# A second written-out order for the engines of an attention and feed-forward kernel, nine more unread products, and one weight block copied by ScalarE

## The chip, the cores and the metric

The kernel runs on one core of a Trainium2 chip. The metric is the device time of one launch in microseconds (us). TensorE does the matrix products, VectorE and ScalarE elementwise work, GpSimd elementwise work and the transfers that add, and SyncE issues the plain transfers.

## The reference

Two parts follow each other. The first is attention over 4 batches of 8 heads, 768 positions and 64 features, in which each query sees the keys less than 16 positions away and, for each block of 32 positions, one summary key (the maximum) with one summary value (the mean).

```python
k_sum = k.reshape(B, H, nb, block, D).max(axis=3)
v_sum = v.reshape(B, H, nb, block, D).mean(axis=3)
scores_all = np.concatenate([scores_l_m, scores_s], axis=-1)   # near keys (masked), then summaries
a = softmax(scores_all)                                        # 1e-9 added to the sum
attn = a @ np.concatenate([v, v_sum], axis=2)
```

The second is a layer of width 2048 with a rational activation on the 3072 x 512 result.

```python
h = x @ w_in
g = (a0 + a1*h + a2*h**2 + a3*h**3) / (1 + |b0|*|h| + |b1|*h**2 + 1e-6)
out = g @ w_out
```

The spread of the inputs is wide, so the kernel carries the operands of the two large products as a high and a low part, and does three products where one would stand.

## The kernel before, in words

**Attention** is done in 48 chunks of 64 queries (names ending in 0 to 47: `sc3`, `ss3`, `pt3`, `pts3`, `av3`). Chunks 0 to 15 go through `early_half` (line 323). Scores of a pair of chunks are made by TensorE (`sc`). VectorE takes the maximum, ScalarE the exponentials (four activations, each with the read of its sum, and one small one), VectorE the reciprocal, GpSimd multiplies (four operations, `ss`; VectorE for chunks 3 and 5), TensorE transposes (`pt`), one engine copies (`pts`), TensorE multiplies by the values (`av`), and `xh` and `xl`, the high and low part of the result, are written by two more operations. `BYDVE` names the copies that VectorE does in place of ScalarE (`C3`: `pts` of chunk 3; `X3`: `xh` of chunk 3). Chunks 0 to 7 need the block means of the values: TensorE sums them (`vs`), ScalarE copies the sums beside chunk 0's values (`vw0`, four copies), and ScalarE and GpSimd copy them on for the other seven chunks (`first_means`, line 253).

**The two layers** run in 96 steps: 6 groups of 512 rows by 16 weight blocks. In a step TensorE does twelve products of the first layer (`h`: high part of x, low part, then the high part with the weights' low part; step 0 does the low part of x last). A dozen operations of ScalarE, VectorE and GpSimd then make the activation: `gh`, its high part, comes from VectorE, and `gl`, its low part, is the last and comes from GpSimd. Three steps later (`LAG`) twelve products of the second layer (`po`) use both. "Step 5's second layer" below is the twelve `po` products that read `gh0_5` and `gl0_5`.

**Weights** come as 64-bit numbers in 16 blocks of 1 MB (`wr0` to `wr15`) through SyncE and pass six stages in `w_split` (line 480): ScalarE scales, GpSimd turns one byte, VectorE joins the bits, then the high part is copied, and the low part is made. `MODE` has a letter per block for the last two: with `c` ScalarE copies and VectorE subtracts; with `b` a converting transfer of GpSimd copies, ScalarE negates and an adding transfer of GpSimd makes the low part; `e` is the same with the copy on ScalarE. Blocks 2, 6, 7, 8, 10 and 11 use an adding transfer. It stands in GpSimd's list of work and needs some us to land.

**Order.** Each engine does its work strictly in the order of the text, and that order is the token list `ORDER`: `a3` is the next stage of chunk 3, `b1` a pair's scores, `v` and `m` the means, `w8` the next stage of weight block 8, `h`, `g`, `q`, `P` the parts of a step, `K`, `Q`, `V`, `A`, `W` the transfers. `SLOTS` says which of a tile's buffers each use takes, and was made for that list. `VSP` names the PSUM bank of the two sums of means.

**Unread products.** `FILL` puts products that nobody reads ahead of a chunk's scores (`b`) or transposes (`t`) on TensorE; they are 480 columns of bf16, written to the bank that the chunk then overwrites.

Of the kernel before, what the change touches and what calls it, by code (L numbers as in the profile page):

```python
# [57 lines left out]
FILL = {'b0': 3, 'b4': 3, 't2': 5, 't0': 5}  # L58
SLOTS = {'wm': '1010', 'ta': '10101010101010101010101010101010101010101010101010101010101010101010101010101010101010101010101010', 'tq': '01101010101010101010101010101010100101010101010101101010101010101010101010101010101010110101010101', 'st': '010101010111100110011011', 'gh': '012011201201201201201201201201201201201201201201201201201201201201201201201201021021021021021201201201', 'h': '01010101010101010101010101010101010100100100101010101010101101100110101010100101001001010101001010110101101010101010101010', 'ks': '0101', 'o': '012301231032101320132013201320132013201', 'gl': '0120201201201201201201201201201201201201201201201201201201201201201201201201201201201201201201201201', 'sm': '012301320132102310321032103213012301231023102301', 'p': '0123201302301320133231023232313012131012031230202023010312101302012010131230313231203132132132303101021302130', 'xl': '0101010', 'tu': '010101010101010101010101010101010101010101010101010101010101010101010101010101010101010101010101010', 'a': '0101010101011011011001010100100101011101111010101001000100000011111011010101011101010010001011101111010010101010101010101010101010', 'xh': '0110101', 'pts': '010100101010100111010111011010100101011010100100', 'vs': '01'}
# [9 lines left out]
K1 Q0 K0 K3 S K2 W0 w0 d3 d0 w0 d1 d2 b0 a1 a0 Q1 a1 w0 W1 a1 a0 w0 a1 w1 B I b2 a4 b3 a0 a2 a4 W2 w1 a0 a2 w0 a7 F w1 c a4 V7 V4 a1 V3 b1 a2 w2 V6 w0  # L69
w1 a5 V5 a1 w2 w1 a2 a4 V0 w2 a7 w1 a0 v4 v5 v6 a7 k9 a5 v0 a6 V2 a7 v3 V1 A9 v8 v2 A8 a6 w2 v7 a0 v1 v9 m0 a3 a2 W3 a3 a0 w2 a5 a5 W5 m4 a4 m2 a6 m5  # L70
a2 k8 m3 a6 a0 b4 W4 a0 a4 a3 m1 a5 a5 a3 a9 w3 a1 a3 a1 a8 a5 a6 a3 a3 a7 a8 m6 a1 a6 w3 a7 G a2 w3 V8 a5 a2 a3 a8 w5 a4 a6 m7 w2 a7 a6 a6 a5 a2 a4
w5 a3 a7 w3 w4 a9 w3 a7 a4 a8 h0 V9 w5 g0 w4 w4 L11 h1 w3 a9 w5 n4 n3 g0 W6 q0 g0 w4 q0 W7 g1 w5 n0 w5 g0 A10 n1 a9 a8 a9 a8 a9 g1 g1 g0 q1 q1 g0 g1
g1 A11 h2 g2 W9 a9 g2 w4 q2 w4 W8 n2 n5 o P3 a9 g2 w6 q2 g1 a9 g2 h3 w6 g3 D11 a8 w6 w7 g2 w7 w6 g3 a8 g2 w6 w9 h4 P4 L10 q3 a8 w7 V11 g4 b5 P5 q3 a10
q4 g4 g3 g3 g3 w8 w6 h5 q4 w9 a11 w7 g4 w8 h6 g3 A12 a10 g5 P6 w8 g4 g4 g5 q5 w9 w8 g4 w7 w7 L13 W10 a11 q5 a11 P7 g5 w10 D10 w8 g5 V10 a10 h7 w10 g5
g6 w10 w10 a11 D13 q6 g6 w8 g5 w9 g6 w9 q6 L12 w9 a11 w10 g6 a10 P8 a10 g7 a10 a11 g6 w10 g6 W11 A13 h8 w11 g7 q7 a10 D12 a11 q7 w11 a10 W12 g7 P9 a10
g8 w12 w11 a11 g7 g7 k12 h9 W13 k13 q8 g8 w11 g7 q8 w12 g8 a11 w11 w12 w11 g9 g8 g8 P10 g8 w12 W15 g9 b6 A14 w13 h10 A15 w13 a13 g9 a13 q9 a12 q9 w13
# [700 lines left out]
```

## Time and profile before

| | us |
|---|---|
| median of 3 runs | 631.09 (631.05 to 631.6) |
| profiled execution | 630.29 |
| its span, first to last instruction | 628.4 |
| TensorE busy in the span | 615.1 |
| VectorE busy | 556.5 |
| ScalarE busy | 453.4 |
| GpSimd busy | 251.2 |

The span is what the rows below divide; 1.9 us of the execution lie around it. The first product of the first layer starts at 40.06 us. Before it chunks 0 to 7 of the attention are done, beside the first weights; after it TensorE runs the 96 steps with the rest of the attention between them.

### The profile page before, as it was taken

The page shows a single profiled execution, that of the slowest core. Times are in us where ns is not written, and L with a number is a line of the kernel's source. Part 1 is how long each engine was busy: PE and PEld are TensorE (multiplying, and loading weights), DVE is VectorE, ACT ScalarE, POOL GpSimd, SP SyncE. Part 2 cuts the span into 40 slices and gives each one's busy share as a digit, 9 for nine tenths or more (in the row PEclk, how much of TensorE's full clock was granted, in tenths as well). Part 3 has the DMA queues.
Part 4 walks back from the last instruction along what each step waited for, and adds up shares of the span by engine and source line. Part 5 has one row for each costly group of instructions (what it writes and reads, how often), then busy time and mean ns, then how long its engine had stood idle before and what let it go on. Part 6 is the DMA issues. An engine that isn't in the chain of part 4 may idle for free.

```text
span 628.4 us, 12096 instructions
## 1 busy us (share of the span) xinstructions
PE 615.1 (98%) x4204; PEld 491.8 (78%) x4204; DVE 556.5 (89%) x1068; ACT 453.4 (72%) x1007; POOL 251.2 (40%) x351
## 2 busy tenths in 40 slices
PE   8899989999999999999999999999999999999997
PEld 4577767778888888878888888888888887878885
DVE  4999999999999898899887999999798897867895
ACT  3998989777968677867785777858777675846553
POOL 0974664771424622334353133354143532221231
PEclk9799999999999999999999999999999999999999
DMA  8998799313342740423353433434413122100001
GB/s 331 340 310 329 221 263 284 118 32 103 121 148 83 213 126 18 159 86 119 111 164 101 143 92 113 145 101 134 136 55 105 59 65 74 68 0 2 0 1 67
DMA packets 52180, 80.78 MB, mean 129 GB/s; under 512 B 6472, under 2 KB 33000, under 8 KB 50200
## 3 DMA queue, kind: packets, MB, share of 16 engines
q1 hardware_dynamic: 50328, 74.87, 36.6%
q0 software_dynamic: 1424, 4.92, 3.5%
q8 instruction: 33, 0.54, 0.4%
q10 hardware_dynamic: 368, 0.22, 0.1%
q14 instruction: 27, 0.22, 0.1%
HBM read 60.33 MB, written 14.75 MB: 119 GB/s over the span
## 4 chain that ended last, share of the span: by engine, by line
PE 79%; DVE 9%; ACT 4%; DMA 3%; POOL 2%; issue 1%; SPq 0%; POOLq 0%; DVEq 0%; ACTq 0%
PE po L162 35%; PE h L162 35%; PE sc L162 4%; PE av L162 4%; DVE tu L162 3%; DVE tq L162 2%; ACT ta L162 2%; DMA w<-wr 1%; PE pt L162 1%; DVE gh L162 1%; DMA kres<-in_kraw_dram 1%; POOL gl L162 1%; DVE wr L162 1%; DMA kr<-in_kraw_dram 1%; DVE sm L162 1%
## 5 line engine op out<-in xcount | busy, mean ns | idle before, releaser
L162 POOL TENSOR_TENSOR gl<-tu,ta 128x512 fp32r<-128x512 f32 x95 | 129.0, 1359 | 325.5 <-DVE tu L162 235.0
L162 PE MATMUL po<-w,gh 128*128 128x512 f32 x384 | 119.9, 394 | 0.0
L162 PE MATMUL po<-wearly,gh 128*128 128x512 f32 x384 | 119.6, 393 | 0.0
L162 PE MATMUL h<-xh,w 128*128 128x512 f32 x384 | 97.8, 393 | 1.7 <-DMA w<-wr 1.5
L162 PE MATMUL h<-xh,wearly 128*128 128x512 f32 x384 | 97.0, 392 | 0.6 <-ACT xh L162 0.6
L162 POOL TENSOR_SCALAR ss<-ss,sm 128x120 f32<-128x120 f32 x184 | 85.8, 487 | 17.1 <-DVE sm L162 9.2
L162 ACT ACTIVATE ta<-tq,cs 128x512 f32<-128x512 f32 x96 | 69.3, 722 | 31.8 <-DVE tq L162 30.2
L162 DVE SCALAR_TENSOR_TENSOR gh<-tu,cs,ta 128x512 fp32r<-128x512 f32 x96 | 77.1, 805 | 11.4 <-ACT ta L162 7.3
L162 PEld LDWEIGHTS h<-xh,w 128*128 128x128 f32 x384 | 71.0, 188 | 18.8 <-DMA w<-wr 2.0
L162 PEld LDWEIGHTS h<-xh,wearly 128*128 128x128 f32 x384 | 71.3, 188 | 16.8 <-ACT xh L162 0.7
L162 ACT ACTIVATE ta<-h,cs 128x512 f32<-128x512 f32 x95 | 64.7, 681 | 26.1 <-POOL gl L162 25.6
L162 PEld LDWEIGHTS po<-wearly,gh 128*128 128x128 f32 x384 | 71.2, 188 | 15.7 <-issue 1.1
L162 PEld LDWEIGHTS po<-w,gh 128*128 128x128 f32 x384 | 71.0, 188 | 15.0 <-issue 0.3
L162 ACT ACTIVATE sq<-h 128x512 f32<-128x512 f32 x72 | 42.0, 583 | 52.5 <-PE h L162 31.6
L162 DVE SCALAR_TENSOR_TENSOR tu<-tu,cs,tq 128x512 f32<-128x512 f32 x96 | 74.9, 780 | 3.4
L162 PE MATMUL po<-wearly,gl 128*128 128x512 f32 x192 | 75.1, 391 | 1.2 <-POOL gl L162 1.2
L162 PE MATMUL po<-w,gl 128*128 128x512 f32 x192 | 75.1, 391 | 0.0
L162 ACT ACTIVATE tu<-h,cs 128x512 f32<-128x512 f32 x96 | 74.5, 776 | 0.0
L162 DVE SCALAR_TENSOR_TENSOR tu<-tu,cs,h 128x512 f32<-128x512 f32 x96 | 71.0, 742 | 1.5
L162 DVE TENSOR_TENSOR tu<-tu,h 128x512 f32<-128x512 f32 x96 | 65.1, 678 | 7.8 <-ACT tu L162 6.6
L162 DVE SCALAR_TENSOR_TENSOR tq<-tq,gh 128x512 f32<-128x512 f32 x96 | 68.6, 714 | 1.8
L162 DVE SCALAR_TENSOR_TENSOR tq<-sq,cs,ta 128x512 f32<-128x512 f32 x72 | 53.4, 743 | 13.7 <-ACT ta L162 13.6
(105 smaller groups left out, 914.1 us busy)
## 6 DMA issues: line engine op xcount, KB each, us to landing
wr<-in_wio_dram SPq DMA_DIRECT2D x15, 1024.0 KB
cross<-tb SPq DMA_DIRECT2D x32, 256.0 KB
vw<-in_vpad_dram SPq DMA_DIRECT2D x42, 192.0 KB
kw<-in_kwin_dram SPq DMA_DIRECT2D x40, 192.0 KB
pts<-cross SPq DMA_DIRECT2D x96, 64.0 KB
out_dram<-o SPq DMA_DIRECT2D x23, 256.0 KB
qw<-in_qw_dram SPq DMA_DIRECT2D x40, 128.0 KB
kr<-in_kraw_dram SPq DMA_DIRECT2D x12, 384.0 KB
```

Source lines behind the costliest of these rows:

```text
L162: out = getattr(self.engine, name)(*args, **kw)
```

## The change

Five tables are altered and no function.

- `ORDER` is another list with the same tokens, and `SLOTS` belongs to it. A large part of the rows of each engine stands in another place up to about step 80; the end of the list is as before.
- `FILL` has `t5: 9`, so nine unread products stand ahead of chunk 5's transposes, beside the sixteen of before.
- `BYDVE` has `X15`, so VectorE writes `xh` of chunk 15 in place of ScalarE.
- `MODE` has `e` in place of `b` for weight block 8, so ScalarE copies its high part, in place of a converting transfer of GpSimd.
- `VSP` puts the first sum of means in a bank of the other pool.

```diff
-BYDVE = 'C2 C3 C4 C6 X0 X13 X2 X3 X6'
+BYDVE = 'C2 C3 C4 C6 X0 X13 X15 X2 X3 X6'
-FILL = {'b0': 3, 'b4': 3, 't2': 5, 't0': 5}
+FILL = {'b0': 3, 'b4': 3, 't2': 5, 't0': 5, 't5': 9}
-VSP = 'ao'
+VSP = 'oo'
 ORDER = """
-K1 Q0 K0 K3 S K2 W0 w0 d3 d0 w0 d1 d2 b0 a1 a0 Q1 a1 w0 W1 a1 a0 w0 a1 w1 B I b2 a4 b3 a0 a2 a4 W2 w1 a0 a2 w0 a7 F w1 c a4 V7 V4 a1 V3 b1 a2 w2 V6 w0
+K0 K1 d0 S K3 d3 K2 I Q0 d2 B d1 W0 Q1 W1 w0 V7 w0 b0 c a1 W2 w0 A8 b2 a1 w0 a0 w0 a1 b3 a2 k9 V6 a0 a1 w0 a2 a4 w1 a7 A9 V4 a1 a2 V1 a0 F a4 k8 w2 w1
...
-MODE = 'ccgcaceebcehpccc'
+MODE = 'ccgcaceeecehpccc'
```

Three places of the list are shown as the engines get it. The first is ScalarE shortly before the means of the values are copied. `pts0` is the copy of chunk 0's transposes, `vw0<-vs0` are the four copies of the means, `ss` the exponentials of a chunk, and `wearly<-wr1` the copy of weight block 1. Before:

```order
L162 ACTIVATE sm6_439<-sm6_439 128x4
L162 COPY pts0_474<-pt0_404 120x512
L162 COPY vw0_102<-vs0_414 24x128 x4
L162 ACTIVATE ss3_488,sm3_489<-sc3_339,sm3_489 128x120 x4
L162 ACTIVATE sm3_489<-sm3_489 128x4
L162 COPY vr0_116<-vw0_102 24x512
```

And now:

```order
L162 COPY pts0_477<-pt0_430 120x512
L162 ACTIVATE ss3_451,sm3_452<-sc3_372,sm3_452 128x120 x4
L162 ACTIVATE sm3_452<-sm3_452 128x4
L162 CAST wearly_105<-wr1_148 128x1024
L162 ACTIVATE ss5_349,sm5_350<-sc5_257,sm5_350 128x120 x4
L162 ACTIVATE sm5_350<-sm5_350 128x4
L162 COPY vw0_102<-vs0_446 24x128 x4
```

The exponentials of chunks 3 and 5 and the copy of block 1 have moved ahead of the copies of the means.

The second place is GpSimd around the adding transfer of weight block 8, `w8<-wr8`. `gl0_4` and `gl0_5` are the low parts of steps 4 and 5, `ss10` and `ss11` the multiplications of chunks 10 and 11. Before, where the first `w8<-wr8` is the converting transfer and the second the adding one:

```order
L162 DMA w8_1105<-wr8_866 128x1024
L162 TENSOR_TENSOR gl0_4_960<-tu0_4_981,ta0_4_979 128x512
L162 DMA wearly_105<-wr7_777 128x1024
L162 TENSOR_SCALAR wr10_1112<-wr10_1112 128x1024
L162 TENSOR_SCALAR ss11_1048<-ss11_1048,sm11_1049 128x120 x4
L162 DMA w8_1105<-wr8_866 128x1024
L162 TENSOR_TENSOR gl0_5_1045<-tu0_5_1081,ta0_5_1079 128x512
L162 TENSOR_SCALAR ss10_1018<-ss10_1018,sm10_1019 128x120 x4
```

And now:

```order
L162 DMA wearly_105<-wr7_865 128x1024
L162 TENSOR_TENSOR gl0_4_958<-tu0_4_1027,ta0_4_1025 128x512
L162 TENSOR_SCALAR ss11_1041<-ss11_1041,sm11_1042 128x120 x4
L162 TENSOR_TENSOR gl0_5_1003<-tu0_5_1093,ta0_5_1091 128x512
L162 TENSOR_SCALAR ss10_1065<-ss10_1065,sm10_1066 128x120 x4
L162 DMA w8_1139<-wr8_973 128x1024
L162 TENSOR_SCALAR wr10_1128<-wr10_1128 128x1024
```

The adding transfer stands behind step 5's low part and chunk 10's multiplications; it stood ahead of both. The converting transfer is gone.

The third place is TensorE in the same stretch, from the last products of step 7 (`h0_7`) to those of step 8 (`h0_8`); `pt` are transposes, `av` products with the values. Before:

```order
L162 MATMUL h0_7_1141<-xh0_509,wearly_105 128x512 x4
L162 MATMUL pt11_1185<-ident_92,ss11_1048 120x128 x4
L162 MATMUL po0_0_879<-wearly_105,gh0_5_1044 128x512 x2
...
L162 MATMUL po0_3_882<-wearly_105,gl0_5_1045 128x512
L162 MATMUL pt10_1208<-ident_92,ss10_1018 120x128 x4
L162 MATMUL h0_8_1231<-xh0_509,w8_1105 128x512 x4
```

And now:

```order
L162 MATMUL h0_7_1166<-xh0_565,wearly_105 128x512 x4
L162 MATMUL pt11_1192<-ident_92,ss11_1041 120x128 x4
L162 MATMUL pt10_1202<-ident_92,ss10_1065 120x128 x4
L162 MATMUL po0_0_907<-wearly_105,gh0_5_1002 128x512 x2
...
L162 MATMUL po0_3_910<-wearly_105,gl0_5_1003 128x512
L162 MATMUL av11_1225<-pts11_1219,vw1_103 64x64 x8
L162 MATMUL av10_1244<-pts10_1222,vw0_102 64x64 x8
L162 MATMUL h0_8_1266<-xh0_565,w8_1139 128x512 x4
```

Chunk 10's transposes stand ahead of step 5's second layer, and the two products with the values ahead of step 8's first layer, where they stood behind it.

## Rows read from the trace of the kernel before

**Rows 1.** The page: busy time, share and instructions of each engine.

```profile
PE 615.1 (98%) x4204; PEld 491.8 (78%) x4204; DVE 556.5 (89%) x1068; ACT 453.4 (72%) x1007; POOL 251.2 (40%) x351
```

**Rows 2.** Waits of TensorE from 95 us on: who for whom, us, times, longest.

```profile
PE po L162 <- POOL gl L162: 0.3, 1, 0.3
```

**Rows 3.** TensorE in order of time: start, us, operation, [idle before <- releaser].

```profile
53.05 0.50 PE L162 MATMUL po<-wearly,gl 128*128 128x512 f32 x1 [0.42 <-POOL gl L162]
...
84.32 0.50 PE L162 MATMUL po<-wearly,gl 128*128 128x512 f32 x1 [0.52 <-POOL gl L162]
...
90.73 1.19 PE L162 MATMUL h<-xh,w 128*128 128x512 f32 x4 [1.55 <-DMA w<-wr]
```

**Rows 4.** The chain of work that ended last, in order of time: start, us, what.

```profile
31.79 1.39 PE sc L162 x34
...
81.38 9.30 DMA w<-wr
...
134.44 2.97 PE po L162 x12
...
140.49 2.72 PE po L162 x12
```

**Rows 5.** Stretches of 2 us: busy time of each engine, granted clock, transfers.

```profile
core 0: us, PE busy (x) PEld busy (x) DVE busy (x) ACT busy (x) POOL busy (x), PEclk, DMA share, GB/s
18.00:20.00 2.00, 0.56 (x1) 0.10 (x1) 1.89 (x3) 1.97 (x12) 1.91 (x4) 0.74 1.07 340
...
26.00:28.00 2.00, 2.00 (x70) 1.89 (x72) 1.89 (x7) 1.11 (x7) 2.00 (x5) 1.00 1.10 343
...
78.00:80.00 2.00, 2.00 (x10) 1.68 (x9) 2.00 (x5) 2.00 (x3) 1.90 (x4) 1.00 0.86 164
```

**Rows 6.** ScalarE in order of time, the opening.

```profile
11.42 1.16 ACT L162 ACTIVATE wr<-wr 128x1024 f32<-128x1024 f32 x1 [9.39 <-DMA wr<-in_wio_dram]
...
17.55 0.35 ACT L162 ACTIVATE ss<-sc,sm 128x120 f32<-128x120 f32 x1
...
19.14 0.34 ACT L162 ACTIVATE ss<-sc,sm 128x120 f32<-128x120 f32 x1
...
29.72 1.10 ACT L162 COPY vw<-vs 24x128 f32<-24x128 f32 x4
```

**Rows 7.** TensorE in order of time, the opening.

```profile
28.45 1.19 PE L162 MATMUL pt<-bias,hot 96*128 96x480 bf16 x5
29.47 0.60 PE L162 MATMUL pt<-ident,ss 128*120 128x128 f32 x4
...
35.59 0.65 PE L162 MATMUL pt<-ident,ss 128*120 128x128 f32 x4
36.17 0.69 PE L162 MATMUL av<-pts,vr 120*64 120x64 f32 x16
...
40.06 2.14 PE L162 MATMUL h<-xh,wearly 128*128 128x512 f32 x8 [0.60 <-ACT xh L162]
```

**Rows 8.** VectorE in order of time.

```profile
38.19 0.74 DVE L162 CAST xh<-av 128x256 fp32r<-128x256 f32 x2
...
81.24 0.75 DVE L162 SCALAR_TENSOR_TENSOR tu<-tu,cs,tq 128x512 f32<-128x512 f32 x1
```

**Rows 9.** GpSimd in order of time.

```profile
75.71 1.29 POOL L162 TENSOR_TENSOR gl<-tu,ta 128x512 fp32r<-128x512 f32 x1 [1.46 <-DVE tu L162]
...
82.14 2.13 POOL L162 TENSOR_TENSOR gl<-tu,ta 128x512 fp32r<-128x512 f32 x1
84.26 1.39 POOL L162 TENSOR_SCALAR ss<-ss,sm 128x120 f32<-128x120 f32 x4
```

**Rows 10.** Adding transfers of blocks 6 and 7, then of blocks 8 and 10: issue to landing.

```profile
DMA to landing us min/median/max: 4.7/5.0/5.3
...
DMA to landing us min/median/max: 8.1/8.7/9.3
```

**Rows 11.** SyncE's issues beside the adding transfer of block 8.

```profile
81.73 0.33 SPq L162 DMA_DIRECT2D wr<-in_wio_dram  x1
```

More of the change, by code (lines that the diff above doesn't have):

```diff
@@ new lines @@
+w14 W15 q11 a12 g12 a14 q11 w13 g11 a13 P13 h13 a13 w15 g11 q12 a15 g12 V15 a12 q12 g11 a13 w14 P14 g12 a13 w14 a12 w14 a15 V14 w14 a14 a15 g13 a12
+g12 a14 g12 w14 g13 q13 A16 g12 a14 q13 w15 w15 h14 a15 g13 g13 w15 g13 w15 a14 P15 w15 g14 h15 A17 q14 a14 a14 a15 g13 P16 g14 a15 q14 L20 g15 g15
+g14 q15 q15 g14 h16 g14 b8 g15 a17 g15 A19 g15 g14 g16 a17 q16 q16 h17 g16 a17 g15 g16 g17 P17 P18 g16 g16 q17 g16 q17 h18 g17 A18 f0 a16 D20 f0 h19
+g17 g17 b9 a17 g17 f0 a18 g17 g18 f0 q18 q18 g19 P19 g18 g18 q19 g19 g19 L22 g18 g18 a16 a16 q19 g19 h20 g18 L23 g20 g20 g20 V16 P20 A21 g19 q20 V17
@@ new lines @@
+h40 q39 U20 g39 g38 q39 U23 g39 P41 g39 a24 g40 a29 a26 h41 g40 q40 V25 g40 g39 A30 q40 g40 g40 g39 a26 h42 g41 a28 g41 P42 g40 a29 g42 q41 g42 q42
+q41 P43 g41 q42 a29 a28 h43 V24 z12 b15 a26 g41 g41 g42 g42 V27 z12 z12 a29 a31 g42 z12 a31 L30 L32 V26 A33 g41 g43 a31 a28 A32 h44 g42 a30 P44 q43
+g44 q43 a28 g43 g43 a27 a31 g44 a28 P45 a30 g43 h45 g43 q44 q44 g43 g44 a31 g44 z13 g45 a28 z13 z13 D32 P46 q45 g45 V29 z13 V28 h46 b16 a30 a29 a30
+q45 a30 g44 z14 V31 g45 a32 g45 g45 V30 z14 g44 g46 z14 g46 P47 a30 q46 g45 g46 h47 z14 a33 a32 a31 q46 g46 g47 A35 g46 A34 g46 P48 q47 z15 z15 z15
@@ new lines @@
+f3 q65 g65 g64 g65 f3 g65 g66 a43 f3 g66 a43 q66 g66 a42 q66 g66 g66 h67 V40 g67 q67 P67 a41 g67 g67 A45 q67 P68 g66 g67 a40 g67 g67 a42 h68 a43 h69
+g68 g68 q68 q68 g69 P69 h70 g69 q69 g68 g69 q69 a42 b22 g69 a42 g68 a42 a45 g68 a45 z20 z20 g69 g68 a44 g70 q70 g69 z20 P70 A47 g70 h71 V42 z20 g71
+g71 g71 P71 A46 P72 q71 g70 q71 a44 q70 g71 h72 g70 a42 g70 g70 g72 a45 h73 g71 g72 a43 q72 P73 g71 V43 g73 q72 q73 q73 g72 g73 g72 g73 g72 h74 g72
+P74 g74 g74 h75 g74 q74 a45 q74 z21 b23 g73 g73 z21 a46 a44 h76 g73 V45 P75 z21 g74 a44 g74 a45 g75 g74 g75 a46 q75 a47 g75 g76 q75 g75 a46 a44 a46
@@ new lines @@
+a47 z21 g75 q76 g76 a47 g75 V44 P76 a44 g76 P77 h77 a46 a47 q76 g76 g76 h78 a45 g77 q77 g77 P78 g76 a47 q77 z22 g77 g78 g78 V47 z22 q78 g77 P79 z22
+g77 h79 g78 z22 q78 a46 V46 g77 g79 g78 g78 g78 P80 g79 a47 z23 z23 z23 z23 g79 q79 P81 h80 q79 g80 g79 g79 h81 g80 g80 g79 P82 q80 q80 h82 g80 g81
+g80 q81 f4 g81 f4 q81 g80 h83 f4 g81 g82 g81 g81 f4 q82 g81 g82 g83 g82 q83 g83 q82 g83 g82 g82 P83 q83 P84 g82 h84 P85 g83 g84 g84 q84 g83 g83 g84
+q84 g84 h85 g84 h86 g84 g85 g85 g85 q85 g86 q85 g85 q86 g85 P86 q86 g86 P87 g86 h87 g85 h88 P88 g86 g87 g86 g86 g87 g88 q87 g88 g88 P89 q88 q87 q88
@@ L113 @@
+g88 h89 g87 g87 g87 g87 g89 g88 g89 q89 g88 h90 P90 q89 g89 g89 g89 g90 g90 P91 g90 g89 q90 q90 g90 h91 g91 g91 g91 P92 q91 q91 g91 g90 h92 g90 g91
+g92 g92 g92 q92 g91 q92 h93 g93 g92 P93 h94 g92 g93 g92 q93 g93 q93 g93 g93 g94 g94 P94 q94 g94 g93 h95 q94 g95 P95 g94 P96 g95 g94 g95 q95 q95 g94
+g95 g95 g95 P97 P98 f5 f5 f5 f5
 """
-MODE = 'ccgcaceebcehpccc'
+MODE = 'ccgcaceeecehpccc'
 NHALF = NT // HQ
```

69 lines of the change are left out of this document (25 added, 44 removed).

## The prediction

> **What bounds the kernel now.** I read the page first: TensorE is busy for 98% of the span [rows 1]. It can gain only where it waits, where its clock is low, or where its work gets shorter, and the change takes no work away. So I read its waits next. From 95 us on there are three, together 0.7 us, of which one stands in [rows 2]: from there the kernel is TensorE's work end to end. Between the first layer's start at 40.06 us [rows 7] and 95 us there are again three: 0.42 us for the low part of step 0, 0.52 us for that of step 5, and 1.55 us for the weights of block 8 [rows 3]. The last one is on the chain of waits, with the adding transfer of 9.30 us in front of it [rows 4]. All the rest is the opening of 40 us, where every engine is nearly always at work and TensorE's clock was low for a while: 0.74 granted as the mean of 18 to 20 us, 1.00 again in 26 to 28 [rows 5].
>
> One more thing is to be seen there. VectorE is busy for the whole of 78 to 80 us [rows 5], and so it is in nearly all stretches from 16 to 130 us. A list that leaves VectorE the same work ahead of an operation doesn't bring that operation much earlier, whatever TensorE does.
>
> **The opening.** ScalarE decides when the means are copied. Its first scaling waits for weight block 0 and starts at 11.42 [rows 6]. The identity and the coefficients now come ahead of that block on SyncE's queue; I put 0.4 us on it, 11.8. Up to the copies of the means ScalarE now has three scalings and two block copies at about 1.1, exponentials of seven chunks at 1.59 (the next chunk starts at 19.14 after one at 17.55 [rows 6]), a whole-chunk exponential of 0.6, and two copies of transposes of 0.55: 18.3 us. The copies start at 30.1 at the earliest, against 29.72 before [rows 6]. Chunk 0's transposes now stand on TensorE behind the scores of chunks 3 and 6, chunk 4's transposes and five unread products; ScalarE may wait for them up to 1.3 us. I take half, so 30.8, with 30.1 and 31.4 as ends.
>
> From there to the first layer took 40.06 - 29.72 = 10.34 us before. Three things differ in TensorE's row of work. Two transposes now stand earlier (2 x 0.58, from 35.59 to 36.17 [rows 7]). So do the scores of chunks 8 and 9, 1.39 [rows 4]. The nine unread products are added: five took 1.02 (28.45 to 29.47 [rows 7]), so nine take 1.85. The sum is 9.64, and the first layer starts at 40.4, or 0.4 later (39.7 to 41.0). The nine are counted in full, because by this working nothing keeps TensorE waiting where they stand. If it does wait there, for chunk 5's multiplication on VectorE, they cost nothing and 1.85 is the price without that cover. The Trainium skill, "TensorE: Matmul & The Clock Gate", section "Step-by-step: what each phase is for", says that only weight loads are pulled ahead and products start in the order of the program; by that the nine hold up everything behind them. The five of [rows 7] held up nothing, since the means came later than they ended. By the page the opening is +0.4, by the row -1.4.
>
> **Step 0's low part.** Step 3's first layer now stands between step 2's and step 0's second layer. That is 2.7 us of work, and the wait of 0.42 goes.
>
> **The stretch of weight block 8.** GpSimd's low part of step 5 needs VectorE's operation that started at 81.24 and took 0.75 [rows 8]. In both lists the same VectorE work stands ahead of it (two key sums have changed places with two others), and VectorE has no gap there, so it ends at 82.0 again, give or take half a us. The low part takes 1.29 to 2.13 [rows 9]; the longer one ran beside VectorE's joining of block 9's bits, which now stands earlier, so I take 1.3: 83.3. Chunk 10's multiplication takes 1.39 [rows 9]: 84.7. Only now can chunk 10's transposes end on TensorE (85.0), and step 5's second layer is queued behind them; so are two products with the values and step 8. Before, that layer lost 0.52 and in effect ran from 83.9. With 2.75 for it, 1.15 for the products with the values and 2.1 for two thirds of step 8, TensorE wants block 8's low part at 91.1.
>
> The adding transfer is issued at 84.7, behind chunk 10's multiplication, where it was issued at 81.38 [rows 4]. The rows give 4.7 to 5.3 us to landing for blocks 6 and 7, and 8.1 to 9.3 for blocks 8 and 10 [rows 10]; block 8's had the load of a weight block issued 0.35 us after it [rows 11]. Now block 12's load follows about 1.4 us after the issue, when VectorE has subtracted block 9. I take 7.5, nearer to the slow rows: it lands at 92.2 and TensorE waits 1.1 (0 to 2.9 by the two ends). Before, it went on at 90.73 with the two products with the values (1.15) still to do, which is 91.88 in the new order. So by the end of step 8 the change stands at 92.2 - 91.9 = +0.3, opening and step 0 included, since VectorE sets the pace; the ends are -1.3 and +2.6. The mode `e` itself gives ScalarE 1.1 us of copying and takes a transfer from GpSimd; it is hidden behind step 5's activation, and costs nothing as long as the negation ends before 84.7. I estimate 80.
>
> **Later.** A block of twelve products takes 2.97 after other work and 2.72 after its like [rows 4]: 0.25 a change. The new list has 34 such changes after the start of the first layer, the old one 36: -0.5. Block 11's adding transfer is issued about 4 us later, since its negation now stands behind step 8's activation; step 11's first layer is later by a second layer and a pair's scores, 4.1 us. I put +0.3 on it, between 0 and 2. Chunk 15's `xh` puts 0.37 on VectorE (two took 0.74 [rows 8]) four blocks of products ahead of its use: nothing. The waits after 95 us stay.
>
> **The sum.** +0.3 - 0.5 + 0.3 = +0.1 on the profiled execution's 630.29 us (a span of 628.4 and 1.9 around it): 630.4. The median of the runs is 631.09, 0.8 above the profiled one, so the forecast there is **631.2**, no change that can be measured; about 0.2%, 1.3 us, can be told from none. Its own range is 630 to 632.4.
>
> **Rivals.** *The adding transfer is in time (faster).* At 4.7 to 5.3 us it lands at 89.4 to 90.0, ahead of 91.1. The stretch then ends at 91.1, which is -0.8. If VectorE comes half a us earlier out of the opening, where its key sums start with the first load and not with the third, it is -1.3. With -0.5 for the changes that is -1.8: 629.3, and 628.6 if the nine unread products fall in a wait. For it: block 8's transfer no longer starts beside a load. Against it: the load of block 12 falls inside it. It decides at 6.4 us from issue to landing.
>
> *The adding transfer is as slow as before (slower).* At 9.3 us it lands at 94.0, TensorE waits 2.9, and the stretch ends at +2.1; with -0.5 and +0.3 that is +1.9: 633.0. It decides from 8.6 us on. For it: both rows of this stretch are over 8. Against it: this time the load starts later. The Trainium skill, "DMA: Bandwidth & Descriptors", section "Queues, rings and completion order", has each transfer engine take turns between the queues that have work. By that, 4.7 us of which all but the first 1.4 is shared becomes 1.4 + 2 x 3.3 = 8.0, an estimate from the rows' 4.7, and the time 631.7; the 9.3 beside a load from the start fits it.
>
> *The clock stays low (slower).* TensorE waits for the means between the last sum and 30.8 us. Before, its clock fell after a wait of similar size at 17 to 19 us and came back before 26 [rows 5]. If it falls at the means, some 6.8 us of transposes and products run at 1.2 and not 2.4 GHz, and the opening is 3.4 us longer: 634. Against it: the nine unread products stand close behind.
>
> **How the numbers follow.** The forecast has 0.43, the transfer in time 0.27, the slow transfer 0.19, the low clock 0.11. Faster by over 0.2% takes nearly all of the second and little of the first, 0.27; within 0.2% most of the first and some of the second and third, 0.40; slower the rest, 0.33. The range is 628.8 to 633.8: it holds the first three cases but for their ends, and leaves out most of the low clock.
>
> **What would show it.** In the trace of the changed kernel: the copies of the means at 30.8 and the first layer at 40.4; no wait at step 0's second layer; chunk 10's transposes waiting for GpSimd for about 1.5 us near 84; a wait for `w<-wr` of about 1 us near 91; a granted clock of 1.00 from 26 us on. I am wrong if VectorE has gaps between 43 and 82 us, if TensorE waits after 95 us for more than 1.5 us in all, or if the first layer starts outside 39.5 to 41.5.

## The result and the profile after

| us | before | changed |
|---|---|---|
| median of 4 runs each | 631.35 (631.05 to 633.02) | 637.67 (637.21 to 639.62) |
| profiled execution, its span | 630.29, 628.4 | 639.62, 637.7 |
| first product of the first layer | 40.06 [rows 7] | 44.26 |
| from there to the end of the span | 588.3 | 593.4 |

The ratio is 1.0088 [1.0059, 1.0117]: the change makes the kernel 0.9% slower. The forecast was 631.2, from 628.8 to 633.8, so the time lies outside the range. The profiled execution is the slowest of the four. A second series of the same kernel (told below as a run of its own) had a median of 639.03 and a profiled span of 635.0, with the first layer at 42.67 and 592.3 behind it. The loss is thus in two places, and both stand in both executions: 2.6 to 4.2 us before the first layer, 4.0 to 5.1 us behind it.

The page of the changed kernel answers to [rows 1]. TensorE has 4 us more busy time, although the nine unread products are all that was added to it:

```profile
PE 619.1 (97%) x4213; PEld 496.1 (78%) x4213; DVE 554.7 (87%) x1069; ACT 454.4 (71%) x1007; POOL 252.2 (40%) x350
```

**Behind the first layer.** The waits of TensorE from 95 us on (who for whom, us in all, times, longest) answer to [rows 2]. Before, all three were 0.7 together. Now:

```profile
PE sc L162 <- ACT ss L162: 4.2, 1, 4.2
PE av L162 <- DMA pts<-cross: 0.8, 1, 0.8
PE h L162 <- DVE tu L162: 0.7, 1, 0.7
PE av L162 <- DVE tu L162: 0.6, 2, 0.4
PE po L162 <- POOL gl L162: 0.3, 1, 0.3
```

One wait of 4.2 us is new, and the chain that ended last (start, us, what) leads to its cause:

```profile
100.45 1.72 DVE wr L162
102.17 0.29 issue
102.46 8.15 DMA w<-wr
110.61 0.02 issue
110.63 0.70 DVE w L162
111.32 1.32 DVE tq L162 x2
112.65 0.59 DVE sc L162
...
113.45 1.49 ACT ss L162 x8
114.94 0.04 issue
114.98 2.37 PE sc L162 x33
117.35 4.66 PE h L162 x12
122.01 2.72 PE po L162 x12
```

`w<-wr` is the converting transfer of weight block 11. Behind it VectorE makes the negation for the adding transfer (`w`); behind that, in VectorE's own row of work, stand parts of steps 9 and 10 and the maxima of chunk 12 (`sc`), which ScalarE's exponentials (`ss`) need, and for these the next scores on TensorE wait. The same on the engines, in order of time: SyncE's load of weight block 13, GpSimd's issue of the transfer, VectorE, TensorE.

```profile
101.06 0.33 SPq L162 DMA_DIRECT2D wr<-in_wio_dram  x1
```
```profile
102.46 0.61 POOL L162 DMA_DIRECT2D w<-wr  x1 [1.36 <-DVE wr L162]
```
```profile
110.63 0.70 DVE L162 TENSOR_SCALAR w<-w 128x1024 fp32r<-128x1024 f32 x1 [3.43 <-DMA w<-wr]
```
```profile
114.98 0.56 PE L162 MATMUL sc<-bias,hot 96*128 96x480 bf16 x1 [4.17 <-ACT ss L162]
115.47 1.88 PE L162 MATMUL sc<-kw,qw 64*64 64x120 f32 x32
```

The transfer is issued 1.4 us behind a load of 1 MB and takes 8.1 us. Before, it was issued at 95.09 and took 3.1, and block 13's load came 1.3 us after it (GpSimd's issue, its time to landing, and SyncE's three loads of which block 13's is the first):

```profile
95.09 0.60 POOL L162 DMA_DIRECT2D w<-wr  x1 [2.76 <-ACT sq L162]
```
```profile
DMA to landing us min/median/max: 3.1/3.1/3.1
```
```profile
96.39 1.81 SPq L162 DMA_DIRECT2D wr<-in_wio_dram  x3
```

The wait has an after-effect. In this stretch (us, busy time of PE, PEld, DVE, ACT, POOL, granted clock, transfer share, GB/s) TensorE was granted 0.50, its level of 1.2 GHz:

```profile
116.00:120.00 4.00, 4.00 (x34) 3.12 (x27) 3.62 (x7) 3.08 (x5) 3.39 (x2) 0.50 0.71 236
```

A pair's scores then take 1.88, where they took 1.05 in the trace of before:

```profile
101.74 1.05 PE L162 MATMUL sc<-kw,qw 64*64 64x120 f32 x32
```

A first layer takes 4.66, where a block of twelve products after its like takes 2.72 [rows 4]. Together that is 2.8 us. The sum is 4.17 + 2.8, less the waits of [rows 3] that are gone (0.42 + 0.52 + 1.55): 4.5 of the 5.1 us.

**Before the first layer.** The scores of the second load of queries started at 13.32 in the kernel before:

```profile
13.32 0.40 PE L162 MATMUL sc<-kres,qres 64*64 64x96 f32 x8
```

Now TensorE waits for that load, and ScalarE copies the means late:

```profile
14.00 0.40 PE L162 MATMUL sc<-kres,qres 64*64 64x96 f32 x8 [2.02 <-DMA qres<-in_qfirst_dram]
```
```profile
34.53 1.10 ACT L162 COPY vw<-vs 24x128 f32<-24x128 f32 x4
```
```profile
44.26 2.11 PE L162 MATMUL h<-xh,wearly 128*128 128x512 f32 x8 [0.47 <-ACT xh L162]
```

[rows 6] has the copies at 29.72. From the copies to the first layer it is 9.73 us, against 10.34 before; the opening loses its time ahead of the copies. The stretches answer to [rows 5]:

```profile
12.00:14.00 2.00, 0.00 (x0) 0.00 (x1) 0.70 (x1) 1.89 (x6) 1.09 (x1) 1.00 1.03 434
14.00:16.00 2.00, 2.00 (x66) 1.35 (x66) 1.97 (x5) 1.97 (x7) 0.04 (x1) 0.80 1.06 379
...
18.00:20.00 2.00, 2.00 (x30) 1.54 (x24) 1.80 (x6) 1.97 (x8) 1.69 (x4) 0.50 0.99 364
...
24.00:26.00 2.00, 2.00 (x58) 1.48 (x60) 0.00 (x0) 1.29 (x8) 1.92 (x4) 0.64 0.90 259
```

TensorE does nothing from 12 to 14, and its clock is low from 15.2 to 25.4. From 24 to 26 VectorE does nothing: it waits for scores that TensorE makes at the low clock, behind chunk 2's transposes and five unread products. In the midst of these products TensorE stood still for 1.05 us, and the trace names nothing that it waited for:

```profile
21.56 1.38 PE L162 MATMUL pt<-bias,hot 96*128 96x480 bf16 x3 [1.05 <-issue]
```

VectorE's waits of the opening and ScalarE's longest one behind them:

```profile
13.30 1.23 DVE L162 SCALAR_TENSOR_TENSOR wr<-wr 128x1024 int32<-128x1024 int32 x1 [1.50 <-POOL wr L162]
26.33 0.67 DVE L162 TENSOR_REDUCE sc<-sc 128x4 f32<-128x480 f32 x1 [3.34 <-PE sc L162]
41.23 0.42 DVE L162 CAST xh<-av 128x256 fp32r<-128x256 f32 x1 [1.46 <-PE av L162]
```
```profile
27.36 0.36 ACT L162 ACTIVATE ss<-sc,sm 128x120 f32<-128x120 f32 x1 [2.03 <-DVE sm L162]
```

Before, VectorE waited nowhere from 12.2 to 92 us for more than 0.3. So the busy time of VectorE in the first 125 us is a meter for both losses. First the kernel before, then the changed one (columns as above):

```profile
0.00:125.00 125.00, 116.79 (x1117) 86.28 (x1118) 112.96 (x191) 101.96 (x238) 72.27 (x93) 0.97 0.85 275
```
```profile
0.00:125.00 125.00, 112.95 (x1071) 82.83 (x1072) 105.62 (x180) 98.11 (x231) 70.22 (x89) 0.93 0.84 266
```

VectorE is 7.3 us behind with its work at 125 us, and the span is 9.3 longer. Over the eighteen profiles of the experiments the excess of the span is this deficit plus -0.5 to +2.9 us.

### The profile page after: what moved, and what is told of

The parts are those of the page before. It is cut to its first block, busy times and chain, and to the rows that moved or that the text cites. A ratio compares the mean times of both kernels' runs of the same rounds, so it can differ in the third digit from the quotient of the medians.

```text
span 637.7 us, 12110 instructions
## 1 busy us (share of the span) xinstructions
PE 619.1 (97%) x4213; PEld 496.1 (78%) x4213; DVE 554.7 (87%) x1069; ACT 454.4 (71%) x1007; POOL 252.2 (40%) x350
## 4 chain that ended last, share of the span: by engine, by line
PE 75%; DVE 8%; ACT 6%; DMA 6%; issue 2%; POOL 1%; SPq 0%; POOLq 0%; DVEq 0%; ACTq 0%
PE po L162 33%; PE h L162 33%; PE sc L162 4%; PE av L162 3%; DVE tu L162 2%; DVE tq L162 2%; DMA kr<-in_kraw_dram 2%; ACT ta L162 2%; PE pt L162 2%; DMA w<-wr 1%; DMA qres<-in_qfirst_dram 1%; DVE gh L162 1%; ACT ss L162 1%; DVE wr L162 1%; DMA kres<-in_kraw_dram 1%
## 5 line engine op out<-in xcount | busy, mean ns | idle before, releaser
L162 POOL TENSOR_TENSOR gl<-tu,ta 128x512 fp32r<-128x512 f32 x95 | 131.7, 1387 | 323.1 <-DVE tu L162 260.2
L162 DVE SCALAR_TENSOR_TENSOR gh<-tu,cs,ta 128x512 fp32r<-128x512 f32 x96 | 75.4, 788 | 11.4 <-ACT ta L162 7.4
L162 DVE SCALAR_TENSOR_TENSOR tq<-tq,gh 128x512 f32<-128x512 f32 x96 | 66.3, 691 | 2.1
```

The costliest lines, as they stand in the source:

```text
L162: out = getattr(self.engine, name)(*args, **kw)
```

## The experiments

Each kernel is timed beside the kernel before on the same chip. "Opening" is the start of the first layer, "rest" the span behind it (before: 40.06 and 588.3; changed: 44.26 and 593.4, and 42.67 and 592.3).

**The queries first.** The second queries are loaded ahead of the coefficients and weight block 0.

```diff
-I Q0 d2 B d1 W0 Q1 W1
+I Q0 d2 Q1 B d1 W0 W1
```

> The changed kernel with one move on SyncE's queue: the second load of the first queries stands ahead of the coefficients and of weight block 0, where it stood behind both. Theory A (the queries that land at 13.96 us make TensorE wait 2.02 us, and its clock is then low until 24.9): no wait near 12 us, a granted clock of 1.00 from 14 to 26, and the first layer starts at 39.5 to 41.5 instead of 44.26; with the stall at 110 us unchanged about 633.5 us. Rival B (the nine unread products, and the three operations moved ahead of the copies of the means on ScalarE, make the opening longer): the wait goes, but the first layer starts within 0.7 us of 44.26 and the time stays at 637.

638.07, ratio 1.0097 [1.0066, 1.0129]; opening 42.97, rest 591.5. The wait for the queries is gone, and another stands in its place: weight block 0 lands later, ScalarE scales it later, and TensorE waits for the exponentials behind the scaling. The clock was low again from 16 to 23 us. Order of loads alone doesn't mend the opening.

```profile
15.63 0.36 PE L162 MATMUL sc<-bias,hot 96*128 96x480 bf16 x1 [1.95 <-ACT ss L162]
```

**Unread products in the wait.** The loads stay; ten more unread products stand ahead of the scores that wait for the queries.

```diff
-FILL = {'b0': 3, 'b4': 3, 't2': 5, 't0': 5, 't5': 9}
+FILL = {'b0': 3, 'b4': 13, 't2': 5, 't0': 5, 't5': 9}
```

> The changed kernel with ten more unread products (13 instead of 3) ahead of the scores of chunks 4 and 2, so that TensorE computes while it waits for the late queries: 10 x 0.20 = 2.0 us. Theory A1 (most of the price of the late queries is the low clock after the wait): the granted clock stays at 1.00 to 20 us or longer, the first layer starts 2 to 4 us earlier than 44.26, about 634.5 us. Rival A2 (the price is that the scores come 2 us late, whatever the clock): the first layer stays within 0.7 us of 44.26, and the time at 637.

635.98, ratio 1.0069 [1.0041, 1.0096]. The granted clock is 1.00 through the whole opening, and the first layer starts at 42.26, 2.0 earlier than in the first profile and 0.4 earlier than in the second. By these profiles the low clock is a part of the opening's loss and not all of it; the four profiles compared at the end of this section bear that out.

```profile
14.00:16.00 2.00, 2.00 (x53) 1.21 (x52) 1.91 (x3) 1.97 (x10) 0.00 (x0) 1.00 1.07 389
```

**Block 11 without transfers.** ScalarE copies, VectorE subtracts.

```diff
-MODE = 'ccgcaceeecehpccc'
+MODE = 'ccgcaceeececpccc'
```

> The changed kernel with the high part of weight block 11 copied by ScalarE and its low part subtracted by VectorE; the converting and the adding transfer of this block and VectorE's negation between them are gone. Theory C (VectorE waits 3.43 us for the converting transfer in front of the negation, all of step 9, 10 and chunks 12 and 13 stands behind it, and TensorE waits 4.17 us and then has a low clock): no wait of VectorE near 107, none of TensorE over 1 us near 111, a clock of 1.00 from 112 to 124; 4.2 + about 2.7 us less, 630.5 to 631.5 us. Rival D (TensorE waits there for the scores' buffer because chunk 12's exponentials stand too far behind on ScalarE, transfer or not): a wait of over 2.5 us stays, 635 or more.

637.81 in four runs that lie far apart (633.16 to 638.95), ratio 1.01 [1.0065, 1.0135]; the profiled one is the fastest, with opening 41.36 and rest 589.7. The rest is 2.6 to 3.7 shorter. VectorE's wait is gone, TensorE's is halved, still for chunk 12's exponentials:

```profile
109.97 0.36 PE L162 MATMUL sc<-bias,hot 96*128 96x480 bf16 x1 [2.04 <-ACT ss L162]
```

So half of TensorE's wait is left without any transfer there, and the clock was low for 3.4 us behind it. By the median alone it would be no gain; the trace shows the place mended in part. The opening of one program differs by up to 2.9 us between executions (44.26 and 42.67, and 41.36 here, where the edit doesn't reach the opening), so I compare openings and rests from here on, and one profile's opening tells little.

**Queries first, and block 11 without transfers.** The two edits together.

> The moves of e1 and e3 together. If the two losses are independent they add up: 637.7 - 4.2 - 6.9 = 626.6 us, 0.7% less than the kernel before. Rival (an opening that ends earlier only runs into the next wait, that for weight block 8, so that half or more of the 4 us is given back): 629 to 631.

634.31, ratio 1.0043 [1.0025, 1.006]; opening 43.62, rest 590.0. The rest keeps what block 11 gave; the opening is later than with either alone.

**Without the nine.**

```diff
-FILL = {'b0': 3, 'b4': 3, 't2': 5, 't0': 5, 't5': 9}
+FILL = {'b0': 3, 'b4': 3, 't2': 5, 't0': 5}
```

> The changed kernel without the nine unread products ahead of chunk 5's transposes. Theory V (VectorE is busy nearly without a break from the opening to 112 us, so each microsecond that it waits before that is a microsecond of the kernel; in the changed kernel it waits 1.46 us for the products with the values behind the nine): that wait of VectorE before its cast near 40 us goes, the first layer starts about 1.5 us earlier than in executions with the same waits at 12 and 23 us, 1.5 us less in the time. Rival N (the nine stand in a wait of TensorE and are free): the wait stays as a wait for chunk 5's multiplication, no difference. Rival K (without them TensorE idles there and its clock falls): the granted clock drops near 40 us and the time is longer.

636.36, ratio 1.0079 [1.0053, 1.0105]. From the copies of the means (36.77) to the first layer it is 8.35 us; it is 8.34 or 8.35 in all five kernels without the nine, and 9.73 with them where the clock stayed at 1.00. So the nine cost 1.38 of the counted 1.85, and the median is 1.3 below that of the changed kernel's first series. In this profile the copies themselves came late, with the clock low from 21.0 to 34.7.

**Block 0's bits later.** VectorE takes the maxima of a chunk ahead of joining block 0's bits, for which it waited 1.50 at 13.30.

```diff
-c a1 W2 w0 A8 b2 a1 w0 a0 w0
+c a1 a0 W2 w0 A8 b2 a1 w0 w0
```

> The changed kernel with one move on VectorE: the joining of weight block 0's bits stands behind the maxima of chunk 0 instead of ahead of them. Theory V: the maxima (1.3 us) fill VectorE's wait of 1.50 us for GpSimd's part of block 0 at 11.79 us, so VectorE's busy time up to 125 us rises by about 1.3 and the time falls by about as much. Rival P (the opening is paced by TensorE's scores at its low clock, not by VectorE): the 1.3 us come back as a longer wait of VectorE for the scores near 23 us, and the time stays at 637.

637.94, ratio 1.0097 [1.007, 1.0124]; opening 46.07. That wait went. The one for the scores of chunk 3 stayed (3.32), the first maxima waited 1.79 in place of 0.53, and the 1.46 at 41.23 became 3.01: the clock fell once more, from 37.7 to 41.1 us.

```profile
43.05 0.42 DVE L162 CAST xh<-av 128x256 fp32r<-128x256 f32 x1 [3.01 <-PE av L162]
```
```profile
38.00:42.00 4.00, 4.00 (x27) 2.21 (x28) 1.93 (x6) 1.78 (x6) 3.77 (x5) 0.62 1.00 359
```

**Four edits.** Thirteen unread products in the wait, none of the nine, block 0's bits later, block 11 without transfers.

> Four edits of the changed kernel together: no nine unread products, the joining of block 0 behind chunk 0's maxima, ten more unread products in the wait for the late queries, and block 11 subtracted by VectorE without transfers. Theory V: VectorE's waits up to 112 us fall from 11 to about 3 us, its busy time up to 125 us comes within 1 us of the kernel before (112.96), and the time within 1.5 us of it, 630 to 633 us. Rival: the waits are replaced by others (for ScalarE, for the scores), the time stays at 635 or more.

633.49 (10 runs), ratio 1.0023 [0.9999, 1.0047]; opening 41.74, rest 589.6, the granted clock 1.00 in the whole run. Of the 6.3 us between the medians above 4.2 are back, and with no low clock anywhere the opening is still 1.7 later than before.

**The letter alone.** The old list with ScalarE's copy of block 8, the part that I put at nothing.

```diff
-MODE = 'ccgcaceebcehpccc'
+MODE = 'ccgcaceeecehpccc'
```

> The kernel before with one part of the change alone: the high part of weight block 8 copied by ScalarE, in place of the converting transfer. By the prediction's step the copy (1.1 us) is hidden and costs nothing, and GpSimd's queue loses a transfer: within 1 us of the kernel before. Rival: ScalarE has no 1.1 us to spare between 79 and 88 us, its operations for step 5 come later and with them the second layers, 1 us or more slower.

634.37 (10 runs), ratio 1.004 [1.0009, 1.0072]; opening 39.95, rest 594.4 in the profile, an execution 1.8 above the median. So the letter is not free. Block 8's adding transfer was issued at 81.75 and took 9.9 us (before: 81.38 and 9.3), TensorE waits 2.61 where [rows 3] has 1.55, and the clock is low for 3.4 us behind that. Everything behind is 1.5 later, so block 11's converting transfer is issued at 96.65, 0.23 ahead of block 13's load and not 1.3; it took 7.9, and VectorE waits 3.79 in the same place as with the new list, TensorE 1.74 behind it for a low part:

```profile
91.73 1.30 PE L162 MATMUL h<-xh,w 128*128 128x512 f32 x4 [2.61 <-DMA w<-wr]
```
```profile
104.56 0.69 DVE L162 TENSOR_SCALAR w<-w 128x1024 fp32r<-128x1024 f32 x1 [3.79 <-DMA w<-wr]
```

The mechanism behind the first layer thus needs neither the new list nor the new opening: a shift of 1.5 us against a load is enough.

**Scores first.** On TensorE, the scores of chunks 3 and 6 go ahead of chunk 2's transposes and its unread products.

```diff
-a1 a2 a5 a0 a4 a2 a4 b1 a7 w1
+a1 a2 a5 a0 a4 b1 a2 a4 a7 w1
```

> The changed kernel with one move on TensorE: the scores of chunks 3 and 6 stand ahead of chunk 2's transposes and their five unread products, as they did in the kernel before, and not behind them. Theory T (VectorE's wait of 3.34 us at 23 us is for these scores, which TensorE computes late because it stands in front of chunk 2's transposes at a low clock; the opening's length comes from there): that wait falls under 1.2 us, VectorE's busy time from 12 to 46 us rises by 2 us or more, the first layer starts 2 to 3 us earlier, 2 to 3 us less in the time, 635. Rival S (TensorE's total work at its low clock is what counts, in whatever order): the wait moves to the next operation that waits for TensorE, and first layer and time stay within 0.7 us.

638.03, ratio 1.0083 [1.0057, 1.011]; opening 44.41. VectorE's wait of 3.34 becomes two, the second for the transposes that now come later: 2.91 in all, with the clock low from 21 to 28 us.

```profile
24.40 0.67 DVE L162 TENSOR_REDUCE sc<-sc 128x4 f32<-128x480 f32 x1 [0.91 <-PE sc L162]
...
27.34 0.69 DVE L162 COPY pts<-pt 120x512 f32<-120x512 f32 x1 [2.00 <-PE pt L162]
```

**Block 13's load later.** The changed kernel, with nothing altered but the place of one load on SyncE, behind another transfer. It tells a transfer that is slow by itself from one that is slow beside the load.

```diff
-g9 w11 g8 P10 W13 q9
+g9 w11 g8 P10 q9
...
-g9 g9 a12 w12 A15 b7 q10
+g9 g9 a12 w12 A15 W13 b7 q10
```

> The changed kernel with the load of weight block 13 moved on SyncE's queue behind the queries and keys of chunks 14 and 15, so that it is issued after the converting transfer of block 11 (102.46 us) and not 1.4 us ahead of it. Theory L (the transfer takes 8.1 us, and not 3 to 5, because the load of 1 MB is in front of it): issue to landing falls to 3 to 5.5 us, VectorE's wait of 3.43 us in front of the negation to under 1 us, TensorE's wait of 4.17 us to about 2; 2 to 4 us less in the time. Rival Q (converting transfers on GpSimd's queue take this long when VectorE is busy, load or not): 7 us or more to landing, and the same time.

635.38 (12 runs), ratio 1.0042 [1.0016, 1.0069]; rest 589.4. The load is issued at 103.58 instead of 101.06, 2.7 us after the transfer's issue, and the transfer takes 4.9 instead of 8.1:

```profile
103.58 0.65 SPq L162 DMA_DIRECT2D wr<-in_wio_dram  x1
```
```profile
105.90 0.69 DVE L162 TENSOR_SCALAR w<-w 128x1024 fp32r<-128x1024 f32 x1 [0.20 <-DMA w<-wr]
```
```profile
110.25 0.36 PE L162 MATMUL sc<-bias,hot 96*128 96x480 bf16 x1 [0.98 <-ACT ss L162]
```

VectorE's 3.43 became 0.20, TensorE's 4.17 became 0.98, and the clock stayed at 1.00 there. The eight profiles with the load and the transfer as in the changed kernel have rests from 590.7 to 593.4, so 589.4 lies below all of them. This settles why the transfer was slow, and 3.2 us of TensorE's wait with the low clock behind it. About 1 us of the wait and 1.1 us of the rest against before are left.

**Five edits; the opening's edits and the load.** Both have the scores first, none of the nine, and thirteen unread products in the wait; the first has block 11 without transfers, the second the load of block 13 later.

> The changed kernel with the scores of chunks 3 and 6 ahead of chunk 2's transposes, no nine unread products, ten more in the wait for the late queries, and block 11 subtracted by VectorE without transfers. If VectorE's waits up to 112 us are what the changed list costs, the first layer starts at 40 to 41 us and the time is 630 to 632 us, no longer distinguishable from the kernel before. Rival: TensorE's wait for the scores' bank near 110 us, which block 11 did not explain, keeps it at 633.

> As the five edits, but block 11 keeps its two transfers and VectorE's negation, and the load of weight block 13 is issued later instead. VectorE has 0.5 us less to do than with the subtraction; if the converting transfer lands in 3 to 5.5 us, 629.5 to 631.5 us; if the transfer is slow without the load as well, 633 or more.

634.88, ratio 1.0038 [1.0022, 1.0054], opening 41.04, rest 589.8; and 634.39, 1.0028 [1.0009, 1.0048], opening 43.23, rest 589.1 (12 runs each). The rests agree with the cause. The openings, the same row of work, differ by 2.2 us: in the second the clock was low again from 21 to 28 us. No version of the opening that I made brings it back to 40.

**The loads in the old order.** The new list, but the first loads as before, so that the queries and block 0 land as before.

```diff
-K0 K1 d0 S K3 d3 K2 I Q0 d2 B d1 W0 Q1 W1 w0 V7 w0 b0 c
+K1 Q0 K0 d0 K3 S d3 K2 d2 d1 W0 Q1 W1 w0 B I V7 w0 b0
```

> The changed kernel with the first loads on SyncE's queue in the order of the kernel before (first queries behind the first keys, weight block 0 and the second queries ahead of the coefficients and the identity), and the preparation of the coefficients on VectorE accordingly later, behind the maxima of chunk 0. Theory O (the opening of the changed list is longer because its first loads land later: the second queries' scores begin at 13.9 to 15.2 us in all kernels with its load order, at 13.3 in the kernel before; ScalarE's scaling of block 0 at 12.1 to 13.2 instead of 11.4): scores of the second queries at 13.4 or earlier, the scaling at 11.5, the copies of the means 1 to 2 us earlier than the 34.5 of the changed kernel, 1 to 2 us less in the time, 636. Rival (the order on the engines, above all the scores of chunks 3 and 6 behind the transposes and the unread products, decides): the loads land earlier, the copies stay at 33.5 to 35, and the time at 637.

638.22 (7 runs), ratio 1.0076 [1.0047, 1.0105]; opening 43.68. ScalarE's first scaling starts at 11.46, as in [rows 6], and still the copies of the means come at 33.95. So the old loads alone don't bring the means back. It isn't a clean test of the order on the engines: in this kernel VectorE waits 1.48 us for the coefficients, which now come late, and the clock was low for 3.4 us.

**The letter alone, with the loads later.** The kernel of the letter, with the loads of blocks 13 and 15 behind another transfer.

> The kernel before with the part of the change on weight block 8 alone (ScalarE copies), and the loads of weight blocks 13 and 15 moved on SyncE's queue behind the queries and keys of chunk 14. Theory L (what made that part 2.6 us slower is that block 11's converting transfer was issued 0.2 us ahead of these loads and not 1.3): the transfer lands in 3 to 5.5 us, VectorE's wait of 3.79 us near 101 goes, and the time is 631 to 632.5 us, as the kernel before. Rival (ScalarE's additional copy is the price): the wait goes or not, but the time stays at 634.

642.34, ratio 1.0118 [1.0084, 1.0152]. The transfer took 3.0 us, as expected, but the load came too late: GpSimd waited 6.98 us for block 13 itself. The time says nothing on the letter.

```profile
114.71 1.08 POOL L162 TENSOR_SCALAR wr<-wr 128x1024 int32<-128x1024 uint8 x1 [6.98 <-DMA wr<-in_wio_dram]
```

**Before, with block 11's load later.** To take the load away beside block 8's adding transfer of [rows 4].

> The kernel before with the load of weight block 11 moved on SyncE's queue behind the queries and keys of chunk 13, so that it is issued about 1.6 us behind block 8's adding transfer and not 0.35. Theory L: that transfer lands in 5 us instead of 9.3, TensorE's wait of 1.55 us for block 8 and VectorE's of 0.92 go; 0.9 us less, 630.5 to 631 us. Rival: the load then falls into the rest of the transfer all the same and the wait stays; no difference.

632.56, ratio 1.0005 [0.9977, 1.0032]. The load moved by 0.13 us only (81.73 in [rows 11], now 81.86) and the transfer took 9.6: this tested nothing.

**The new list, mended.** Old loads, none of the nine, block 13's load later.

> The changed kernel with three edits: the first loads in the order of the kernel before, no nine unread products, and the load of weight block 13 later. If loads and the nine are what the opening costs and the load beside the converting transfer the rest, 637.7 - 1.5 - 1.4 - 2.3 = 632.5 us, within 1 us of the kernel before. Rival: the opening stays at 43 us or more and the time at 634 or more.

634.51, ratio 1.0021 [1.0, 1.0042]; opening 42.01, rest 590.5.

**Before, with block 8's adding transfer earlier.** Its negation and its issue stand one operation earlier on ScalarE and GpSimd; no part of the change is in it.

> The kernel before with block 8's adding transfer issued earlier: on ScalarE its negation changes places with block 10's scaling, and on GpSimd the transfer stands ahead of chunk 11's multiplication. It is then issued at about 79.7 us, 2 us ahead of block 11's load (81.7) and not 0.35. Theory L (the load close by is what makes the transfer take 9.3 us): it lands in 5 us or less, TensorE's wait of 1.55 us and VectorE's of 0.92 us go; chunk 11's multiplication and step 5's low part come 0.5 us later; 0.3 to 0.9 us less than the kernel before. Rival (the transfer takes 8 us or more there for another reason): TensorE still waits over 1 us for block 8, and the time is the same or 0.5 us longer.

632.12, ratio 1.0001 [0.9981, 1.0021]. Issued at 79.92, 2.2 us ahead of the load, it still took 9.0; a load of keys stood near. TensorE's wait of 1.55 is gone, since the transfer landed earlier, and the total is no shorter. That fits VectorE's row setting the time in this stretch; the run doesn't show more.

**The changed kernel again.**

> The changed kernel once more, unchanged, in more executions and with a second profile. If block 11's converting transfer and the opening are both properties of the list and not of one execution: a wait of VectorE of 2.3 us or more in front of the negation near 107, a wait of TensorE of 3 us or more near 110, the first layer at 42.5 us or later, a median of 637 to 638.5 us. If one of them was an accident of the one profiled execution, it is missing here.

639.03, ratio 1.0114 [1.0095, 1.0133]. Both losses are there again, the opening with a low clock of 3.4 us in place of 10.2:

```profile
108.78 0.69 DVE L162 TENSOR_SCALAR w<-w 128x1024 fp32r<-128x1024 f32 x1 [3.14 <-DMA w<-wr]
```
```profile
113.13 0.56 PE L162 MATMUL sc<-bias,hot 96*128 96x480 bf16 x1 [3.90 <-ACT ss L162]
```

Four profiles share this opening: the two of the changed kernel, that of block 11 without transfers, and that of block 13's load later. They tell two parts of its loss apart. The scores of the second queries start at 14.00, 15.16, 13.87 and 15.05 us, against 13.32 before. From there to the first layer it is 30.3 us in the first, whose clock was low for 10.2 us, and 27.5, 27.5 and 27.6 in the others, with 3.4 us of low clock. So 6.8 us more of low clock cost 2.8 here. With unread products in the wait, and the clock at 1.00 throughout, it is 27.1.

No kernel of these is faster than the kernel before. The choice of `xh` of chunk 15 on VectorE, the bank of the sums and the tiles' buffers were not tried singly.

## Why the prediction was wrong, step by step

**Block 11: "I put +0.3 on it, between 0 and 2".** This is the step that failed behind the first layer, by about 7 us (4.17 of wait and 2.8 of low clock). I looked at the block's adding transfer and asked when TensorE needs its result. I didn't ask what the converting transfer in front of it does to VectorE. A wait in VectorE's row holds up all that stands behind it, here chunk 12's maxima, which have nothing to do with block 11. Nor did I lay SyncE's loads beside it, as I did for block 8: in the new list VectorE joins block 11's bits later in the row, so the issue moved from 1.3 us ahead of a load to 1.4 behind one. Two of my own signs of being wrong came true ("if TensorE waits after 95 us for more than 1.5 us in all": 4.2 in one wait; and the first layer outside 39.5 to 41.5). Shown by moving one load (wait 4.17 to 0.98, rest 2.9 to 4.0 shorter), and from the other side by the letter alone, which brings the collision into the old list. The last 1 us of the wait is not the load's.

**"The mode `e` itself ... costs nothing".** Wrong on the old list: 1.004. ScalarE had caught up with the copy by 83.1 us; the price is block 8's transfer, which is issued 0.37 later and lands 1.0 later, and the shift behind it. What it costs in the new list was not tried by itself.

**The copies of the means "so 30.8".** The second step that failed: they came at 34.53 and 32.94. ScalarE's amount of work was right: 18.3 counted, and 34.53 - 12.11 (its first scaling) - 3.8 of waits = 18.6. The waits were not: 0.65 allowed, 3.8 found (0.29, 0.99 for weight block 2's load, 2.03 for the maxima, 0.51 for chunk 0's transposes). I counted what ScalarE does and added one wait, and didn't follow what VectorE and TensorE owe it, nor when the second queries land (13.96, after 7.98 us, with the identity, the coefficients and block 0 ahead of them).

**"opening and step 0 included, since VectorE sets the pace".** The premise fits the rows, the conclusion doesn't: VectorE's operation for step 5, which I put at 82.0 again, ended at 85.3. VectorE sets the pace, and so its own waits count in full; it has some 7 us of them in the new opening, as with 1.50, 3.34 and 1.46 above. I assumed that the same work ahead means the same time, which holds only while that engine never waits. The claim that a later opening is caught up was wrong with it.

**The low clock.** As a rival I put it at the means, with "the nine unread products stand close behind" against it, and gave it 0.11. It fell earlier, behind the wait for the queries, and once more at 114.2, behind the wait for chunk 12. A price of 3.4 us for 6.8 us of low clock was near the right size (2.8 there, and 2.8 in the opening by the four profiles).

**What was right.** From the copies to the first layer: 9.64 forecast, 9.73 measured. The closeness is luck: the nine cost 1.38 and not 1.85, and the other terms were off by as much the other way (7.79 counted, 8.35 measured). Step 0's wait went. The wait of 1.5 us at chunk 10's transposes didn't come; TensorE reached them at 87.34 without one. At block 8 the rival in which the transfer is in time came true: issued at 88.14, landed in 5.5, at 93.6, and the products that read it started at 94.29 without a wait; I had let it decide at 6.4 us. Block 12's load followed 1.2 us after the issue. The Trainium skill, "DMA: Bandwidth & Descriptors", section "Queues, rings and completion order", has each transfer engine take turns between queues with work; by the estimate of 8.0 that I drew from it, the transfer would have landed at 96.1 and TensorE would have waited 1.9. The row speaks against that estimate (5.4 to 5.6 in all fifteen profiles of the new list), and the 8.1 against 3.1 of block 11 is more than a half share explains, which by the same estimate makes 6.2 of 3.1 at most. VectorE has no gap over 0.3 us between 43 and 82, as forecast; it was the stretch next to it on both sides that lost.

**What stays open.** With the clock at 1.00 in the whole opening the first layer still comes 1.0 to 2.2 us late (41.04, 41.74, 42.26), although the opening of before had a low stretch itself [rows 5]. In these three the scores of the second queries start at 14.65, 14.71 and 15.18, which is 1.3 to 1.9 later than before and of the size of the loss. That this is the cause isn't shown: in the two kernels with the old loads they start at 13.4 and 13.3, and the first layer still comes at 43.68 and 42.01, with VectorE's wait for the coefficients in place of the other. Queries early with no other load late was not tried. The order of TensorE's and VectorE's work, which hand chunks 2, 3, 0 and 6 to each other, may have a share; each single move that I made only moved the wait. TensorE's stop in the midst of chunk 2's unread products, 0.7 to 2.5 us in six profiles, has no cause in the traces. Nor is it shown why TensorE waits 2.0 us for chunk 12's exponentials where block 11 has no transfers, and 1.0 where only the load is moved. On ScalarE, the two exponentials and the copy ahead of the means explain at most 1.0, because the sums of the values end on TensorE at about 33.5. That was not tried.

## What to carry to other kernels

When a hand-made order is changed, lay every transfer beside the loads that will be issued around it, and for every instruction that waits for a transfer list what stands behind it on its own engine: the work that is held up may be of another stage altogether. For an engine that sets the pace, equal work ahead is not equal time; count its waits, for which its busy time up to a fixed moment is a short test. A wait on TensorE can cost a good part of its length again at the low clock (2.8 us behind the one of 4.2), and unread products are worth their time where TensorE would wait anyway, as at the queries, not where it has work.

## What the runs showed of the hardware

- A converting transfer of GpSimd for block 11 takes 3.0 to 3.1 us where the next load of 1 MB is issued 1.3 to 1.9 us after it or no load is near, 3.9 to 4.9 where it comes 2.4 to 3.4 us after, and 7.1 to 8.1 where the load was issued 1.3 to 1.4 us before it (eight executions); 7.9 where it came 0.23 after. The times at 1.3 and at 2.4 after don't line up, so the distance alone isn't the law.
- Adding transfers of blocks 6 to 11 took 4.5 to 5.8 us where the nearest load of 1 MB was issued 0.95 us or more after them, or 3.8 or more before, and no load of keys within 1.2 us. They took 7.8 to 10.1 with a load of 1 MB from 2.6 us before to 0.6 us after, 6.1 and 6.2 with one 3.3 us before, and 7.4 to 9.0 with only a load of keys within 1.2 us (block 6 in the new list, and the block 8 that is issued earlier). One took 6.9 with neither near.
- TensorE's clock fell to 0.50 after the wait of 2.0 us at 12 us and after the one of 4.2 at 111, and stayed there for 10.2 and 6.8 us; in a second execution of the same program, for 3.4 in the opening. Ten unread products in the first wait kept it at 1.00. Near 110 us it fell behind waits of 1.75 and 2.04 us, and not behind ones of 2.09 and 2.17 (the two kernels of several edits without transfers for block 11), so the length of a wait alone doesn't tell.
